# Scores and probability transposes of an attention kernel, from 64 x 64 and 128 x 128 array tiles to row tiles of 64 x 128

## The chip, the core and the metric

The kernel runs on one core of a Trainium2 chip. The metric is the device time of one execution in microseconds (us). The core has TensorE (PE; its weight loads are shown apart as PEld), VectorE (DVE), ScalarE (ACT), GpSimd (POOL) and the queue from which transfers are issued (SP). TensorE writes its results to PSUM, which has eight banks of 512 fp32 columns per partition; ACT and DVE copy them from there to SBUF.

## What is computed

```python
scores = (1.0 / np.sqrt(D)) * np.matmul(q, k.transpose(0, 1, 3, 2))   # B, H, S, D = 4, 8, 576, 64
bias = np.maximum((psi_rel / psi_i)[..., None] @ w1 + b1, 0.0) @ w2   # of the positions alone
scores = scores + bias.transpose(2, 0, 1)[None, :, :, :]
attn = np.exp(scores - np.max(scores, axis=-1, keepdims=True))
attn = attn / (np.sum(attn, axis=-1, keepdims=True) + 1e-09)
x = np.matmul(attn, v)                       # then (B * S, H * D) = (2304, 512)
h = x @ moe_w_in;  x = (h - np.tanh(h)) @ moe_w_out
h = x @ moe2_w_in; x = (s * np.maximum(h, 0.0) ** 2 + b) @ moe2_w_out
```

All of it is fp32.

## The kernel before

The program has three stages: the position bias (matmuls `b`, line 259), attention, and two feed-forward layers (matmuls `h`, line 312, and `a`, line 550). The change is in attention.

Attention works on 16 pairs (two heads of one batch). A pair `i` has five row blocks `t`: blocks 0 to 3 are 128 query rows of both heads, and block 4 is the last 64 rows of both heads, one head on partitions 0 to 63 and the other on 64 to 127. A loop over `n` runs 80 of these blocks (and three iterations more) as a pipeline that is written out by hand: iteration `n` emits the division of block `n - 2` by its sum (`emit_norm`, POOL, line 422, output `pn`), the scores of block `n` (`emit_score`, TensorE, line 383, output `s`), the exponentials of block `n - 1` (ACT, line 405), the bias and row minimum of block `n` (`emit_bias`, DVE, line 391), the reciprocal of block `n - 1` (DVE, line 413), the transposes of block `n - 3` (`emit_transpose`, TensorE, line 432, output `t`), their copies to `pt` (`emit_parts`, ACT and DVE, lines 444 to 451), some matmuls with the values (`emit_pv`, TensorE, line 462, output `o`), and at two of five iterations the copy of a finished `o` (DVE, line 469). Every engine runs its instructions in this order.

At 16 iterations a `weights_tick` is put at the end, which unpacks a piece of feed-forward weights: on DVE three instructions (lines 130, 139 and 142), on ACT two, on POOL one (line 87). They stand at these `n`:

```python
TK = [*range(15, 63, 4), 66, 70, 74, 78]
```

How the matmuls use the 128 x 128 array of TensorE:

- Scores of a head and row block: the contraction of 64 is split off as a row tile, the 576 keys are two halves of 288 that use the two row tiles (`c`), and the query rows go in two column tiles of 64. So four matmuls of 64 x 64 weights and 288 columns make a set that runs together. The trace shows two instructions for each fp32 matmul, so a head has two sets of four.
- Transposes: nine blocks of 128 x 128 of `pn`, which is the weight operand; the identity is the moving operand. Three blocks share a PSUM bank; there are three banks.
- Values: column tiles of 64, two heads side by side (128 x 64).

PSUM: two buffers of two banks for the scores, three banks for the transposes, one for `o`. A score tile can be written again when DVE has read it (line 391), a bank of the transposes when ACT or DVE has copied it.

Of the kernel before, what the change touches and what calls it, by code (L numbers as in the profile page):

```python
# [10 lines left out]
F32 = mybir.dt.float32  # L11
# [5 lines left out]
PSUM = bass.MemoryType.PSUM  # L17
DRAM = bass.MemoryType.DRAM

B, H, S, D = 4, 8, 576, 64  # L20
# [38 lines left out]
def tile_kernel(ctx, tc, qk, vd, wcat, wts, sb, ltab, psib, ipsi8, out):  # L59
    nc = tc.nc  # L60
# [13 lines left out]
    ident = const.tile([128, 128], F32, name="ident")  # L74
# [111 lines left out]
    with ExitStack() as c0:  # L186
# [40 lines left out]
        for n in range(NG + 2):  # L227
# [18 lines left out]
            if n < NG:  # L246
# [3 lines left out]
                f = 512 - y  # L250
# [85 lines left out]
    with ExitStack() as ca:  # L336
        sp = ca.enter_context(tc.tile_pool(name="sp", bufs=2, reuse_waits="tile"))
        pp = ca.enter_context(tc.tile_pool(name="pp", bufs=4, reuse_waits="tile"))
        np_ = ca.enter_context(tc.tile_pool(name="np_", bufs=3, reuse_waits="tile"))
        gp_ = ca.enter_context(tc.tile_pool(name="gp_", bufs=3))  # L340
        s_ctx = ExitStack()
        ps_s = s_ctx.enter_context(tc.tile_pool(name="ps_s", bufs=2, space=PSUM, side="right", reuse_waits="tile"))
        ps_t = ca.enter_context(tc.tile_pool(name="ps_t", bufs=3, space=PSUM, reuse_waits="tile"))
        ps_o = ca.enter_context(tc.tile_pool(name="ps_o", bufs=1, space=PSUM, reuse_waits="tile"))


# [3 lines left out]
        periods = [(i, t) for i in range(len(pairs)) for t in range(5)]  # L350
# [14 lines left out]
        s_t, raw_t, p_t, n_t, sums, tr_t, unit_t, o_t = {}, {}, {}, {}, {}, {}, {}, {}  # L365

        def heads_of(x):

            t = periods[x][1]
            return [(0, 8, 2)] if t == 4 else [(0, 2 * t, 0), (1, 2 * t + 1, 1)]  # L370

        def emit_score(x):
            i, t = periods[x]
            q, kk = qk_t[i]
            for j, _, e in heads_of(x):
                s = s_t[x, j] = ps_s.tile([128, 2, 512], F32, tag="s", name="s")
                for ee in ((e,) if e < 2 else (0, 1)):
                    o = s if e < 2 else s[ee * 64:ee * 64 + 64]
                    n = IT[t][1]
                    for c in range(2):  # L380
                        h = slice(c * 64, c * 64 + 64)
                        for r in range(0, n, 64):
                            nc.tensor.matmul(o[r:r + 64, c, 0:288], q[h, ee, t * 128 + r:t * 128 + r + 64], kk[h, ee],  # L383
                                             start=True, stop=True)

        def emit_bias(x):
            i, t = periods[x]
# [26 lines left out]

        def emit_norm(x):

            pn = n_t[x] = np_.tile([128, 9, 128], F32, tag="pn", name="pn").rearrange("p j n -> p (j n)")
            sm = sums.pop(x)
            for j, _, e in heads_of(x):
                p = p_t.pop((x, j))  # L420
                for a, b, c in ([(0, 512, 640), (512, 576, 576)] if j else [(0, 576, 0)]):
                    nc.gpsimd.tensor_scalar(out=pn[:, c:c + b - a], in0=p[:, a:b], scalar1=sm[:, j:j + 1],  # L422
                                            scalar2=0.0, op0=ALU.mult, op1=ALU.add)

        def emit_transpose(x):
            pn = n_t.pop(x)
            nb = 5 if periods[x][1] == 4 else 9
            for g in range(0, nb, 3):
                pm = tr_t[x, g] = ps_t.tile([128, 3, 128], F32, tag="t", name="t")
                for j in range(g, min(g + 3, nb)):  # L430
                    c = min(128, 128 * 4 + 64 - 128 * j) if nb == 5 else 128
                    nc.tensor.transpose(pm[0:c, j - g], pn[:, j * 128:j * 128 + c], ident)  # L432

        def emit_parts(x):

            i, t = periods[x]
            u = int(t > 1)
            if (i, u) not in unit_t:
                unit_t[i, u] = gp_.tile([128, 9, 320], F32, tag="pt", name="pt")
            pt = unit_t[i, u]  # L440
            if t < 4:
                c0 = t % 2 * 128
                for copy, g in ((nc.scalar.copy, 0), (nc.vector.tensor_copy, 3), (nc.scalar.copy, 6)):
                    copy(pt[:, g:g + 3, c0:c0 + 128], tr_t.pop((x, g)))  # L444
                return
            a, b = tr_t.pop((x, 0)), tr_t.pop((x, 3))
            for e, copy in ((0, nc.scalar.copy), (1, nc.vector.tensor_copy)):
                h = slice(e * 64, e * 64 + 64)
                copy(pt[:, 5 * e:5 * e + 3, 256:320], a[:, :, h])
                copy(pt[:, 5 * e + 3, 256:320], b[:, 0, h])  # L450
                copy(pt[h, 4, 256:320], b[0:64, 1, h])

        def emit_pv(i, u, j):

            r0, n = UNITS[u]
            v = v_t[i]
            if j == 0:
                o_t[i, u] = ps_o.tile([128, 512], F32, tag="o", name="o")[:, 0:n]
            o = o_t[i, u]
            for e in range(2):  # L460
                h = slice(e * 64, e * 64 + 64)
                nc.tensor.matmul(o[h], v[:, e, j], unit_t[i, u][:, 4 if j == 4 else 5 * e + j, 0:n], start=(j == 0), stop=(j == 4))  # L462

        def emit_out(i, u):
            hp, b = pairs[i]
            r0, n = UNITS[u]
            del unit_t[i, u]
            xo = sp.tile([128, 320], F32, tag="xo", name="xo", bufs=3)[:, 0:n]
            nc.vector.tensor_copy(xo, o_t.pop((i, u)))
            nc.sync.dma_start(out=x1_d[hp][:, b * S + r0:b * S + r0 + n], in_=xo)  # L470

# [10 lines left out]
        for n in range(NK + 6):  # L482
# [6 lines left out]
            if now(2):  # L489
                emit_norm(n - 2)  # L490
            if now(0):
                emit_score(n)
# [7 lines left out]
            if now(3):  # L500
                emit_transpose(n - 3)
                emit_parts(n - 3)
            for i, u, js in PV.pop(n, []):
                for j in js:
                    emit_pv(i, u, j)
                if js[-1] == 4:
                    emit_out(i, u)
# [13 lines left out]
    with ExitStack() as cb:  # L521
# [52 lines left out]
        for n in range(len(seq) + LAG):  # L574
# [15 lines left out]
            if n < len(seq):  # L590
                c, f = seq[n]
# [69 lines left out]
```

## Time and profile before

| what | us |
|---|---|
| median of 3 runs | 1104.89 (1104.89 to 1104.98) |
| span of the profiled execution, first to last instruction | 1102.9 |
| time around the span (median less span) | 2.0 |
| PE busy | 1091.7, 99% of the span |
| DVE busy | 635.9 (58%) |
| ACT busy | 484.4 (44%) |
| POOL busy | 319.9 (29%) |
| busy on scores (PE, line 383) | 89.9 |
| busy on transposes (PE, line 432) | 89.6 |
| busy on values (PE, line 462) | 95.0 |

The profiled execution is given by its span; its time from outside is not listed apart, and the median of the runs stands for it. Busy time of PE is the time in which some matmul is in flight, their ends included, so it says that TensorE had work, not that it was at its peak. The granted clock of TensorE was full (1.00, which is 2.4 GHz) in every window read here.

### The profile page before, as it was taken

The page shows a single profiled execution, that of the slowest core. Times are in us where ns is not written, and L with a number is a line of the kernel's source. Part 1 is how long each engine was busy: PE and PEld are TensorE (multiplying, and loading weights), DVE is VectorE, ACT ScalarE, POOL GpSimd, SP SyncE. Part 2 cuts the span into 40 slices and gives each one's busy share as a digit, 9 for nine tenths or more (in the row PEclk, how much of TensorE's full clock was granted, in tenths as well). Part 3 has the DMA queues.
Part 4 walks back from the last instruction along what each step waited for, and adds up shares of the span by engine and source line. Part 5 has one row for each costly group of instructions (what it writes and reads, how often), then busy time and mean ns, then how long its engine had stood idle before and what let it go on. Part 6 is the DMA issues. An engine that isn't in the chain of part 4 may idle for free.

```text
span 1102.9 us, 17963 instructions
## 1 busy us (share of the span) xinstructions
PE 1091.7 (99%) x6856; PEld 836.6 (76%) x6856; DVE 635.9 (58%) x1239; ACT 484.4 (44%) x1003; POOL 319.9 (29%) x438
## 2 busy tenths in 40 slices
PE   9999999999999999999999999999999999999998
PEld 6555555555578888889888888888888888888897
DVE  8866787787659942223322399998343343343343
ACT  8977777777735432222222255553222222222222
POOL 0155666676715530001200046435030020010000
PEclk9999999999999999999999999999999999999999
DMA  7957546253145010010100265600010020010010
GB/s 284 317 176 227 175 149 226 77 179 130 38 187 198 15 58 1 1 58 20 58 1 1 96 210 210 200 30 20 19 59 1 1 77 1 1 58 1 0 40 20
DMA packets 41335, 99.65 MB, mean 90 GB/s; under 512 B 5024, under 2 KB 11552, under 8 KB 41248
## 3 DMA queue, kind: packets, MB, share of 16 engines
q1 hardware_dynamic: 40960, 98.24, 26.2%
q8 instruction: 54, 0.88, 0.3%
q14 instruction: 33, 0.27, 0.1%
q10 hardware_dynamic: 288, 0.26, 0.1%
HBM read 73.41 MB, written 25.07 MB: 89 GB/s over the span
## 4 chain that ended last, share of the span: by engine, by line
PE 91%; DVE 2%; DMA 1%; issue 1%; ACT 0%; POOL 0%; SPq 0%; ACTq 0%; DVEq 0%
PE h L312 36%; PE a L550 36%; PE o L462 7%; PE t L432 6%; PE s L383 6%; DVE raw L391 1%; DMA qk<-in_qk 1%; DVE wx L142 0%; DVE wx L130 0%; ACT p L405 0%; DVE pt L444 0%; POOL pn L422 0%; DVE wsg L139 0%; SPq L111 0%; DVE mn L391 0%
## 5 line engine op out<-in xcount | busy, mean ns | idle before, releaser
L312 PE MATMUL h<-x,w 128*128 128x512 f32 (+1 forms) x1920 | 420.6, 368 | 0.0
L312 PEld LDWEIGHTS h<-x,w 128*128 128x128 f32 x1920 | 337.4, 188 | 62.4 <-issue 1.3
L550 PE MATMUL a<-ring,w 128*128 128x512 f32 (+1 forms) x960 | 210.1, 368 | 0.0
L550 PE MATMUL a<-w,ring 128*128 128x512 f32 x864 | 209.0, 389 | 0.0
L550 PEld LDWEIGHTS a<-ring,w 128*128 128x128 f32 x960 | 168.3, 189 | 29.9
L550 PEld LDWEIGHTS a<-w,ring 128*128 128x128 f32 x864 | 161.1, 188 | 32.7
L87 POOL TENSOR_TENSOR w<-wx,w 128x512 fp32r<-128x512 f32 x64 | 96.1, 1503 | 219.3 <-ACT w L122 212.4
L333 DVE TENSOR_TENSOR ring<-ring 128x512 fp32r<-128x512 f32 (+1 forms) x160 | 111.1, 695 | 78.8 <-ACT ring L332 78.8
L332 ACT CAST ring<-ring 128x512 fp32r<-128x512 f32 (+1 forms) x160 | 92.3, 577 | 137.9 <-DVE ring L327 98.7
L422 POOL TENSOR_SCALAR pn<-p,sm 128x576 f32<-128x576 f32 (+2 forms) x208 | 129.2, 638 | 43.7 <-DVE sm L413 31.7
L326 DVE TENSOR_TENSOR ring<-ring 128x512 f32<-128x512 f32 (+1 forms) x80 | 54.7, 684 | 147.7 <-ACT ring L325 147.6
L323 DVE TENSOR_TENSOR ring<-h,ring 128x512 f32<-128x512 f32 (+1 forms) x80 | 50.8, 634 | 140.2 <-ACT ring L322 140.1
L391 DVE CUSTOM_DVE_ANT_0 raw<-s,bias 128x576 f32<-128x576 f32 x144 | 103.7, 752 | 36.3 <-PE s L383 32.7
L84 POOL TENSOR_SCALAR x<-xr 128x512 fp32r<-128x512 f32 (+1 forms) x36 | 25.6, 711 | 330.5 <-DMA xr<-x_d 328.5
L322 ACT ACTIVATE ring<-h 128x512 f32<-128x512 f32 (+1 forms) x80 | 44.3, 554 | 164.7 <-PE h L312 164.7
L325 ACT ACTIVATE ring<-h 128x512 f32<-128x512 f32 (+1 forms) x80 | 44.4, 555 | 163.6 <-PE h L312 163.6
L405 ACT ACTIVATE p<-raw,mn 128x576 f32<-128x576 f32 x144 | 110.6, 770 | 6.1 <-DVE mn L391 5.7
L432 PEld LDWEIGHTS t<-ident,pn 128*128 128x128 f32 (+1 forms) x656 | 69.8, 140 | 36.0 <-issue 18.8
L462 PE MATMUL o<-pt,vv 128*64 128x256 f32 (+1 forms) x640 | 95.0, 418 | 0.0
L383 PE MATMUL s<-qk 64*64 64x288 f32 x1152 | 89.9, 418 | 4.6 <-DVE mn L391 4.1
L432 PE MATMUL t<-ident,pn 128*128 128x128 f32 (+1 forms) x656 | 89.6, 279 | 0.7 <-DVE pt L444 0.7
L444 ACT COPY pt<-t 128x384 f32<-128x384 f32 x128 | 60.3, 478 | 54.8 <-PE t L432 54.7
(48 smaller groups left out, 765.6 us busy)
## 6 DMA issues: line engine op xcount, KB each, us to landing
w<-in_wts SPq DMA_DIRECT2D x64, 512.0 KB, 4.7
qk<-in_qk SPq DMA_DIRECT2D x16, 864.0 KB, 5.9
bias_d<-m SPq DMA_DIRECT2D x36, 296.0 KB, 4.4
bias<-bias_d SPq DMA_DIRECT2D x32, 288.0 KB, 4.7
xr<-x_d SPq DMA_DIRECT2D x28, 256.0 KB, 3.0
vv<-in_vd SPq DMA_DIRECT2D x16, 320.0 KB, 3.7
x_d<-o SPq DMA_DIRECT2D x16, 256.0 KB, 2.1
out_x<-o SPq DMA_DIRECT2D x16, 256.0 KB, 2.1
```

The lines of the kernel that those rows point to most:

```text
L87: nc.gpsimd.tensor_tensor(out=lo, in0=raw, in1=hi.bitcast(F32), op=ALU.subtract)
L312: nc.tensor.matmul(h, a, x, start=(k == 0), stop=(k == 3 * KD - 1))
L332: nc.scalar.copy(gh, g)
L333: nc.vector.tensor_tensor(out=gl, in0=g, in1=gh.bitcast(F32), op=ALU.subtract)
L383: nc.tensor.matmul(o[r:r + 64, c, 0:288], q[h, ee, t * 128 + r:t * 128 + r + 64], kk[h, ee], start=True, stop=True)
L391: nc.vector.tensor_tensor_reduce(out=raw.rearrange("p (c j) -> p c j", c=2), in0=s_t.pop((x, j))[:, :, 0:288], in1=bias_t[pairs[i][0], k]. ...
L405: nc.scalar.activation(out=p, in_=raw, func=AF.Exp, scale=-1.0, bias=mn, accum_out=sm[:, j:j + 1])
L422: nc.gpsimd.tensor_scalar(out=pn[:, c:c + b - a], in0=p[:, a:b], scalar1=sm[:, j:j + 1], scalar2=0.0, op0=ALU.mult, op1=ALU.add)
L432: nc.tensor.transpose(pm[0:c, j - g], pn[:, j * 128:j * 128 + c], ident)
L444: copy(pt[:, g:g + 3, c0:c0 + 128], tr_t.pop((x, g)))
L462: nc.tensor.matmul(o[h], v[:, e, j], unit_t[i, u][:, 4 if j == 4 else 5 * e + j, 0:n], start=(j == 0), stop=(j == 4))
L550: nc.tensor.matmul(o, x, y, start=first and j == 0, stop=last and j == 2)
```

## The change

Three things change in attention.

- Scores of blocks 0 to 3: one matmul with 64 x 128 weights takes the place of two with 64 x 64, so a head has two sets of two matmuls. Block 4 keeps 64 x 64.
- Transposes: each block of `pn` is taken as two row tiles, rows 0 to 63 and rows 64 to 127. A transpose has 64 x 128 weights and 64 moving columns. The eight blocks of a row tile go to a bank of its own (`t0`, `t1`), and the two row tiles alternate. The ninth block (the last 64 keys of both heads) goes to a third bank `c`: the first row tile of two row blocks is transposed in the iteration of the second of them, the second row tile in the iteration after.
- Copies: ACT copies the whole bank of row tile 0 (512 columns), DVE that of row tile 1 (512 columns), ACT every second iteration 256 columns of `c`. Before it was 384 columns twice on ACT and once on DVE. POOL writes 64 columns more for block 4, `pn` has 5 buffers in place of 3, `xo` 2 in place of 3.

```diff
-        ps_t = ca.enter_context(tc.tile_pool(name="ps_t", bufs=3, space=PSUM, reuse_waits="tile"))
+        ps_t = ca.enter_context(tc.tile_pool(name="ps_t", bufs=1, space=PSUM, reuse_waits="tile"))
...
-                        for r in range(0, n, 64):
-                            nc.tensor.matmul(o[r:r + 64, c, 0:288], q[h, ee, t * 128 + r:t * 128 + r + 64], kk[h, ee],
-                                             start=True, stop=True)
+                        nc.tensor.matmul(o[0:n, c, 0:288], q[h, ee, t * 128:t * 128 + n], kk[h, ee], start=True, stop=True)
...
-                for a, b, c in ([(0, 512, 640), (512, 576, 576)] if j else [(0, 576, 0)]):
+                for a, b, c in ([(0, S, 0), (448, 512, S)], [(0, S, 0)], [(0, 512, 640), (512, S, S)])[(e + 1) % 3]:
...
+        ROWS = (slice(0, 64), slice(64, 128))
+        def turned(r, out_, in_):
+            nc.tensor.transpose(out_, in_, ident[ROWS[r], ROWS[r]])
+        def emit_tails(r, x):
+            if r == 0:
+                tr_t["c"] = ps_t.tile([128, 2, 2, 64], F32, tag="c", name="c")
+            for k in range(2):
+                turned(r, tr_t["c"][:, k, r], n_t[x + k][ROWS[r], 512:640])
         def emit_transpose(x):
-            for g in range(0, nb, 3):
-                pm = tr_t[x, g] = ps_t.tile([128, 3, 128], F32, tag="t", name="t")
-                for j in range(g, min(g + 3, nb)):
-                    c = min(128, 128 * 4 + 64 - 128 * j) if nb == 5 else 128
-                    nc.tensor.transpose(pm[0:c, j - g], pn[:, j * 128:j * 128 + c], ident)
+            if t in (1, 3):
+                emit_tails(0, x - 1)
+            ab = tr_t[x] = [ps_t.tile([128, 8, 64], F32, tag=f"t{r}", name=f"t{r}") for r in range(2)]
+            for j in range(8 if t < 4 else 5):
+                for r in range(2):
...
+                    turned(r, ab[r][:, j], pn[ROWS[r], c:c + 128])
+            if t in (2, 4):
+                emit_tails(1, x - 2)
...
-                for copy, g in ((nc.scalar.copy, 0), (nc.vector.tensor_copy, 3), (nc.scalar.copy, 6)):
-                    copy(pt[:, g:g + 3, c0:c0 + 128], tr_t.pop((x, g)))
+            for r, copy in ((0, nc.scalar.copy), (1, nc.vector.tensor_copy)):
+                if t < 4:
+                    copy(pt[:, 0:8, c0:c0 + 64], ab[r])
+                else:
+                    copy(pt[:, 4 * r:4 * r + 4, 256:320], ab[r][:, 0:4])
+                    copy(pt[ROWS[r], 8, 256:320], ab[r][ROWS[r], 4])
+            if t in (2, 4):
+                nc.scalar.copy(done[:, 8, 0:256], tr_t.pop("c").rearrange("p k r q -> p (k r q)"))
```

On TensorE this is one iteration before, with the transposes of a block of 128 rows and the scores of the next iteration behind them (an entry is a matmul of the program, the sizes are those of its output, and x is how many in a row).

```order
L383 MATMUL s<-qk 64x288 x8
L432 MATMUL t<-ident,pn 128x128 x9
L462 MATMUL o<-pt,vv 64x256 x4
L383 MATMUL s<-qk 64x288 x8
L432 MATMUL t<-ident,pn 128x128 x9
L462 MATMUL o<-pt,vv 64x256 x4
```

In the changed program the same place, from the last transposes of one iteration to the first of the next, reads as follows; `t_1108` and `t_1109` are the banks of row tile 0 and row tile 1 of one block, `t_1162` and `t_1163` those of the next.

```order
L426 MATMUL t_1108<-ident,pn 128x64
L426 MATMUL t_1109<-ident,pn 128x64
L426 MATMUL c<-ident,pn 128x64 x2
L481 MATMUL o<-pt,vv 64x256 x4
L382 MATMUL s<-qk 128x288 x4
L426 MATMUL c<-ident,pn 128x64 x2
L426 MATMUL t_1162<-ident,pn 128x64
L426 MATMUL t_1163<-ident,pn 128x64
```

The order of scores, transposes and values is as before; the scores are half as many, the transposes twice as many and alternate between two banks, and the `c` transposes come in twos on one row tile, behind the block in one iteration and ahead of it in the next.

On DVE an iteration before is the two bias instructions (`ISA raw,mn` and a read of the minimum), the reciprocal and one copy.

```order
L391 ISA raw,mn<-s,bias 128x576
L391 ISA mn 128x1
L391 ISA raw,mn<-s,bias 128x576
L391 ISA mn 128x1
L413 RECIPROCAL sm<-sm 128x2
L444 COPY pt<-t 128x3x128
```

After the change the same iteration on DVE has the larger copy, of the whole bank of row tile 1, at the same place behind the reciprocal.

```order
L389 ISA raw,mn<-s,bias 128x576
L389 ISA mn 128x1
L389 ISA raw,mn<-s,bias 128x576
L389 ISA mn 128x1
L411 RECIPROCAL sm<-sm 128x2
L464 COPY pt<-t_1421 128x8x64
```

Nothing moved on DVE but the size of the copy and the bank that it frees.

## Rows read from the trace of the kernel before

**Rows 1.** Windows: us; busy of PE, PEld, DVE, ACT, POOL; clock; DMA.

```profile
66.17:298.88 232.71, 229.24 (x2177) 128.08 (x2175) 176.93 (x497) 173.84 (x440) 154.39 (x278) 1.00 0.47 155
```

**Rows 2.** Timeline of PE, one pair: start us, duration us, what, count.

```profile
66.17 1.20 PE L383 MATMUL s<-qk 64*64 64x288 f32 x16
...
69.66 0.72 PE L383 MATMUL s<-qk 64*64 64x288 f32 x8
...
73.20 1.20 PE L383 MATMUL s<-qk 64*64 64x288 f32 x16
74.33 1.20 PE L432 MATMUL t<-ident,pn 128*128 128x128 f32 x9
75.47 1.08 PE L462 MATMUL o<-pt,vv 128*64 128x256 f32 x8
76.48 1.20 PE L383 MATMUL s<-qk 64*64 64x288 f32 x16
...
79.76 1.20 PE L383 MATMUL s<-qk 64*64 64x288 f32 x16
80.89 0.77 PE L432 MATMUL t<-ident,pn 128*128 128x128 f32 x5
81.58 0.65 PE L462 MATMUL o<-pt,vv 128*64 128x256 f32 x4
82.17 0.47 PE L383 MATMUL s<-qk 64*64 64x288 f32 x4
```

**Rows 3.** Tiles t, s, h: count, duration ns min/median/max, first and last start.

```profile
L432 PE MATMUL t<-ident,pn x583: 272/273/332, 67.3 to 297.5; 128*128 128x128 f32 x190, 128*64 128x128 f32 x5
...
L383 PE MATMUL s<-qk x1028: 402/403/453, 66.2 to 298.9; 64*64 64x288 f32 x172
...
L312 PE MATMUL h<-x,w x36: 387/390/499, 304.6 to 319.2; 128*128 128x512 f32 x36
```

**Rows 4.** Groups by form, weight loads: busy us, mean ns of one, idle.

```profile
L432 PEld LDWEIGHTS t<-ident,pn 128*128 128x128 f32 x640 | 68.5, 141 | 36.0 <-issue 18.8 <-POOL pn L422 10.1 <-POOL sm L409 3.9
...
L383 PEld LDWEIGHTS s<-qk 64*64 64x64 f32 x1152 | 35.4, 132 | 52.4 <-DVE mn L391 15.6 <-issue 12.4 <-DVE sm L413 6.3
...
L312 PEld LDWEIGHTS h<-x,w 128*128 128x128 f32 x24 | 4.3, 188 | 1.6 <-issue 0.8
...
L432 PEld LDWEIGHTS t<-ident,pn 128*64 128x64 f32 x16 | 1.8, 111 | 0.0
```

**Rows 5.** Timeline of PEld, the first loads of a score run.

```profile
256.90 0.15 PEld L383 LDWEIGHTS s<-qk 64*64 64x64 f32 x4 [0.38 <-issue]
```

**Rows 6.** Timeline of PE and PEld, transposes behind scores.

```profile
257.68 0.42 PE L383 MATMUL s<-qk 64*64 64x288 f32 x4
...
258.03 0.14 PEld L432 LDWEIGHTS t<-ident,pn 128*128 128x128 f32 x1 [0.44 <-issue]
```

**Rows 7.** Timeline of PE and PEld, transposes behind h.

```profile
307.22 0.39 PE L312 MATMUL h<-x,w 128*128 128x512 f32 x1
307.45 0.27 PE L432 MATMUL t<-ident,pn 128*128 128x128 f32 x1
...
307.22 0.14 PEld L432 LDWEIGHTS t<-ident,pn 128*128 128x128 f32 x1
```

**Rows 8.** Timeline of DVE around a tick, iterations 31 and 32.

```profile
144.11 0.54 DVE L444 COPY pt<-t 128x384 f32<-128x384 f32 x1
144.57 0.68 DVE L130 SCALAR_TENSOR_TENSOR wx<-wx,wsg 128x512 int32<-128x512 int32 x1
...
147.19 0.74 DVE L391 CUSTOM_DVE_ANT_0 raw<-s,bias 128x576 f32<-128x576 f32 x1
147.87 0.08 DVE L391 DVE_READ_ACCUMULATOR2_ANT mn<- 128x1 f32 x1
```

**Rows 9.** Timeline of PE, iteration 33; in brackets the idle time before.

```profile
148.00 1.40 PE L383 MATMUL s<-qk 64*64 64x288 f32 x16 [0.46 <-DVE mn L391]
```

**Rows 10.** Chain that ended last, 100 to 110 us, in order of time.

```profile
96.58 8.98 DMA qk<-in_qk
```

More of the change, by code (lines that the diff above doesn't have):

```diff
@@ L338, in tile_kernel @@
         pp = ca.enter_context(tc.tile_pool(name="pp", bufs=4, reuse_waits="tile"))
-        np_ = ca.enter_context(tc.tile_pool(name="np_", bufs=3, reuse_waits="tile"))
+        np_ = ca.enter_context(tc.tile_pool(name="np_", bufs=5, reuse_waits="tile"))
         gp_ = ca.enter_context(tc.tile_pool(name="gp_", bufs=3))
@@ L415, in emit_norm @@
         def emit_norm(x):
-            pn = n_t[x] = np_.tile([128, 9, 128], F32, tag="pn", name="pn").rearrange("p j n -> p (j n)")
+            pn = n_t[x] = np_.tile([128, 9 * 128], F32, tag="pn", name="pn")
             sm = sums.pop(x)
@@ L420, in emit_norm @@
                 p = p_t.pop((x, j))
-                for a, b, c in ([(0, 512, 640), (512, 576, 576)] if j else [(0, 576, 0)]):
+                for a, b, c in ([(0, S, 0), (448, 512, S)], [(0, S, 0)], [(0, 512, 640), (512, S, S)])[(e + 1) % 3]:
                     nc.gpsimd.tensor_scalar(out=pn[:, c:c + b - a], in0=p[:, a:b], scalar1=sm[:, j:j + 1],
                                             scalar2=0.0, op0=ALU.mult, op1=ALU.add)
-        def emit_transpose(x):
-            pn = n_t.pop(x)
-            nb = 5 if periods[x][1] == 4 else 9
-            for g in range(0, nb, 3):
-                pm = tr_t[x, g] = ps_t.tile([128, 3, 128], F32, tag="t", name="t")
-                for j in range(g, min(g + 3, nb)):
-                    c = min(128, 128 * 4 + 64 - 128 * j) if nb == 5 else 128
-                    nc.tensor.transpose(pm[0:c, j - g], pn[:, j * 128:j * 128 + c], ident)
+        ROWS = (slice(0, 64), slice(64, 128))
[6 more added lines that the diff above has]
+                turned(r, tr_t["c"][:, k, r], n_t[x + k][ROWS[r], 512:640])
+        def emit_transpose(x):
+            i, t = periods[x]
+            if t in (1, 3):
+                emit_tails(0, x - 1)
+            pn = n_t[x]
+            ab = tr_t[x] = [ps_t.tile([128, 8, 64], F32, tag=f"t{r}", name=f"t{r}") for r in range(2)]
+            for j in range(8 if t < 4 else 5):
+                for r in range(2):
+                    if t < 4:
+                        c = j * 128 + j // 4 * 128
+                    else:
+                        c = j * 128 if j < 4 else (512, 448)[r]
+                    turned(r, ab[r][:, j], pn[ROWS[r], c:c + 128])
+            if t in (2, 4):
+                emit_tails(1, x - 2)
+                del n_t[x - 2], n_t[x - 1]
+            if t == 4:
+                del n_t[x]
         def emit_parts(x):
@@ L440, in emit_parts @@
             pt = unit_t[i, u]
-            if t < 4:
-                c0 = t % 2 * 128
-                for copy, g in ((nc.scalar.copy, 0), (nc.vector.tensor_copy, 3), (nc.scalar.copy, 6)):
-                    copy(pt[:, g:g + 3, c0:c0 + 128], tr_t.pop((x, g)))
[L445 to L451, printed above, removed]
+            ab = tr_t.pop(x)
+            for r, copy in ((0, nc.scalar.copy), (1, nc.vector.tensor_copy)):
+                if t < 4:
+                    c0 = t % 2 * 128 + r * 64
+                    copy(pt[:, 0:8, c0:c0 + 64], ab[r])
+                else:
+                    copy(pt[:, 4 * r:4 * r + 4, 256:320], ab[r][:, 0:4])
+                    copy(pt[ROWS[r], 8, 256:320], ab[r][ROWS[r], 4])
+            if t in (2, 4):
+                done = unit_t[i, int(t == 4)]
+                nc.scalar.copy(done[:, 8, 0:256], tr_t.pop("c").rearrange("p k r q -> p (k r q)"))
         def emit_pv(i, u, j):
@@ L461, in emit_pv @@
                 h = slice(e * 64, e * 64 + 64)
-                nc.tensor.matmul(o[h], v[:, e, j], unit_t[i, u][:, 4 if j == 4 else 5 * e + j, 0:n], start=(j == 0), stop=(j == 4))
+                nc.tensor.matmul(o[h], v[:, e, j], unit_t[i, u][:, 8 if j == 4 else 4 * e + j, 0:n], start=(j == 0), stop=(j == 4))
         def emit_out(i, u):
@@ L467, in emit_out @@
             del unit_t[i, u]
-            xo = sp.tile([128, 320], F32, tag="xo", name="xo", bufs=3)[:, 0:n]
+            xo = sp.tile([128, 320], F32, tag="xo", name="xo", bufs=2)[:, 0:n]
             nc.vector.tensor_copy(xo, o_t.pop((i, u)))
```

## Prediction

> **What bounds the kernel now.** I read the busy times of the attention stage first: from 66.17 to 298.88 us PE is busy 229.24 of 232.71 us [rows 1]. So TensorE sets the time, and the other engines matter where it waits for them. The change touches attention alone; the feed-forward layers must take the time that they take now.
>
> Then I read one pair on PE, from 66.17 to 82.17 us, where nothing waits: 16.00 us [rows 2]. Its iterations take, from score start to score start, 3.28 (n mod 5 = 0: 73.20 to 76.48), 3.28 (1), 2.41 (2), 3.49 (3: 66.17 to 69.66) and 3.54 (4). Runs of different length give the steps within a run without their ends. Sixteen score instructions take 1.20 us and eight 0.72: a set of four is 0.24 us. Nine transposes take 1.20, five 0.77: 0.108 each. Eight value instructions take 1.08, four 0.65: 0.215 a set. An iteration of 3.28 us holds 4 x 0.24 + 9 x 0.108 + 4 x 0.215 = 2.79 us of this; the other 0.49 us lies between the runs, about 0.16 at each of three changes of tile shape.
>
> **Why a change of shape costs.** Behind scores, the first weight load of the transposes starts only at 258.03, 0.35 us after the last score set began at 257.68 [rows 6], though that set needs only 0.24. Behind `h`, which has the same 128 x 128 shape as the transposes, the load starts at 307.22 with the last `h` matmul, and the transpose at 307.45 [rows 7]; it loses nothing. So a run with the shape of the run before it starts without the 0.16.
>
> **The change, part by part.**
>
> *Shape.* Scores of blocks 0 to 3 and transposes get one shape. In the 77 iterations with both (n = 3 to 79) 16 have the scores of block 4, which stay 64 x 64. So 61 changes of shape go: 61 x 0.16 = -9.8 us. If transposing itself needs a switch, which no row separates, this is 0.
>
> *First load of the scores.* The first matmul of a run shows what of its weight load is not hidden, as its longest duration over the median: 0.050 us for scores with 64 columns (453 over 403), 0.109 for `h` with 128 (499 over 390), 0.059 for transposes with 128 (332 over 273) [rows 3]. A 64 x 128 score load is ordinary like that of `h`: +0.059 in 61 iterations, +3.6 us (0 if the load starts early). Later loads hide behind sets of 0.24. Half as many score matmuls gain nothing: sets are as long and as many, since the column tiles ran together.
>
> *Transposes.* The price is that of a slot, a pair of row tiles. The moving side is 64 columns, half of 128, so 0.054 of the 0.108. The load has 128 columns still. Loads of transposes are faster than others: 141 ns for 128 columns and 111 for 64 make 0.47 ns a column, whereas 188 for `h` and 132 for 64 columns of scores make 0.88 [rows 4]; 128 columns at 0.47 are 0.060 us, and the unhidden 0.059 says the same. Two loads on different row tiles overlap if they do as in the scores, where four loads (two row tiles by two column tiles) are in flight in 0.15 us [rows 5], hardly more than the 0.132 of one. So a slot is 0.060 us, bound by the load; ends are 0.054 and, with loads at the ordinary rate, 0.109. The two `c` transposes share a row tile and take a slot each. A pair has 8 + 10 + 10 + 10 + 7 = 45 slots: 2.70 us. Before it is 41 x 0.108 = 4.43. Gain 1.73 us, in 16 pairs -27.7.
>
> The section "LDWEIGHTS (loading the stationary operand)" of the page "TensorE: Matmul & The Clock Gate" of the Trainium skill speaks against this: a load takes its columns over 1.2 GHz, whatever its rows, which makes 107 ns here, an estimate from that page, and the sum of PE below about nothing. The rows on `h` agree with it, those on transposes do not.
>
> Sum on PE: -27.7 - 9.8 + 3.6 = -33.9 us, 2.13 a pair, which leaves 13.87. The iterations become 2.81 (0), 2.81 (1), 2.19 (2), 2.90 (3), 3.17 (4).
>
> *What is late next: DVE.* Each tick puts its instructions between the copy of an iteration and the bias of the next, 2.62 us (144.57 to 147.19) [rows 8]. Scores wait behind that for a PSUM buffer, and behind the scores everything on PE: at 148.00 TensorE had waited 0.46 us for the bias [rows 9], whose minimum was read at 147.87 [rows 8]. The stretch of [rows 1] holds 71 iterations, 14 pairs and one of 3.49 us more, which is 227.5 us without waits, so all waits today are 5.2 us. DVE is idle there for 55.8 us, 0.79 an iteration; shorter iterations take 0.43 of that and the larger copy 0.14, and each copying engine has one bank in place of three in turn. So the same tick is felt more. I worked one through by hand, that of iteration 31, counted from its score start. Bias starts at 0.83, each takes 0.68 (147.19 to 147.87), so both are done at 2.2; the reciprocal follows; the copy of 512 columns, for which I take 0.60 from 0.46 for 384 (144.11 to 144.57), ends at 2.87; the tick ends at 5.5. The first bias of iteration 32 ends at 6.2, and iteration 33's first score, due at 2.81 + 2.19 = 5.0, starts at 6.3: 1.3 us late. Its second score and its transposes, which wait for the second bias and for DVE's copy, add 0.3: 1.6 in all. The same by hand for the other places of a tick gives 2.4 at n mod 5 = 2 (2 ticks), 1.5 at 4 (4), 1.0 at 0 (3, without the first tick, which is only a part) and 0 at 3 (3); with three ticks at 1 that is 4.8 + 6.0 + 3.0 + 4.8 = 18.6 us, +13.4 to today's 5.2. Bounds: 4 (DVE's lateness partly absorbed) and 22 (ACT, which has two instructions in a tick, and POOL add their own).
>
> *Transfers.* The load of queries and keys for iteration 20 is issued at 96.58, at the end of iteration 16, and takes 8.98 us [rows 10]; the scores start when it lands. The stretch to there shrinks by up to 0.47 + 0.22 + 0.59 + 0.37 us, all of which turns into waiting: +1.5 us. Other such loads are issued into emptier queues; I count none. SP's order is as before.
>
> *At nothing:* ACT copies 640 columns an iteration in place of 768. POOL has 16 short instructions more; a `pn` is divided an iteration before it is transposed, and that iteration covers them; without it 16 x 0.3 us would show. Five `pn` buffers and two `xo` buffers are used at distances of five and two iterations.
>
> Net: -33.9 + 13.4 + 1.5 = -19.0. From the span of 1102.9 and 2.0 around it, 1104.9 as the median of the runs: **1085.9 us**.
>
> **Rivals.**
>
> 1. *Loads at the ordinary rate.* If a row-tile load takes 0.109 as for `h`, a slot is that: 45 x 0.109 = 4.91 us a pair, 0.48 more than today, +7.6 us. With -9.8 + 3.6 that is +1.4, and DVE stays covered: 1106, no change. This is the skill's rule above as a mechanism of this kernel. For it: `h` and scores; against it: both rows on transposes. 0.11.
> 2. *Row tiles do not overlap (other side).* Transposes might load one after the other: 82 loads. At 0.060 they take 4.92 us and the kernel 1106; at 0.109 they take 8.94, +72 us, and with -6.2 the time is 1171. PE alone is slower from a slot of about 0.107 us up. Against it the overlap in the scores [rows 5]; for it only that no run of before has row-tiled transposes. 0.07, of which 0.05 slower.
> 3. *Everything is given back.* If the single banks made PE wait for the copies in every iteration, by 0.2 us, 77 iterations cost 15 more: 1101. Against it: by the hand count the copy ends at 2.87 and the next transposes are due at 3.8. 0.06; a third of it ends slower or equal.
> 4. *Nothing is given back* by DVE: 1104.9 - 33.9 + 1.5 = 1072.5. Against it the wait in [rows 9], at longer iterations. 0.08.
>
> **Numbers.** The forecast has 0.68, with 1073 to 1098 as its own range (slot 0.054 to 0.068, give-back 4 to 22). The range of 8 in 10 reaches to rivals 4 and 1: 1069 to 1107. A difference under 0.2% (2.2 us) is about what a measurement of this kernel cannot tell from no change. Faster: 0.68 + 0.08 + 0.04 = 0.80; the same: 0.11 + 0.02 = 0.13; slower: 0.07.
>
> **What the changed profile would show.** Right: transposes start in pairs some 0.06 us apart, sixteen in about 0.7 us with their ends; their first load starts while the last score set runs; a pair without ticks takes about 13.9 us; PE's waits for the bias and for DVE's copies grow from a few us to over 10, after ticks. Wrong: slots of 0.11 (rival 1), of 0.12 or more (rival 2), waits for copies in iterations without a tick (rival 3), or a feed-forward stretch that got longer.

## The result, and the profile after

The changed kernel takes 1091.28 us (1090.64 to 1091.71, 4 runs) against 1104.89 for the kernel before: 13.6 us less, a ratio of 0.988 with a 95% interval of 0.986 to 0.989. The forecast was 1085.9, so the direction was right and the gain 5.4 us short.

The first thing to read is one pair in which nothing waits, on the timeline of PE in the changed kernel (start us, duration us, what, count).

```profile
66.03 1.24 PE L382 MATMUL s<-qk 64*128 64x288 f32 x8
67.10 0.66 PE L426 MATMUL t<-ident,pn 64*128 64x64 f32 x16
...
68.92 0.71 PE L382 MATMUL s<-qk 64*64 64x288 f32 x8
...
72.09 1.24 PE L382 MATMUL s<-qk 64*128 64x288 f32 x8
...
74.90 1.24 PE L382 MATMUL s<-qk 64*128 64x288 f32 x8
...
77.69 1.24 PE L382 MATMUL s<-qk 64*128 64x288 f32 x8
78.77 0.47 PE L426 MATMUL t<-ident,pn 64*128 64x64 f32 x10
...
79.88 0.51 PE L382 MATMUL s<-qk 64*128 64x288 f32 x2
```

From 66.03 to 79.88 the pair takes 13.85 us where it took 16.00 [rows 2]; the sum on PE said 13.87. Iterations take 2.89, 3.17, 2.81, 2.79 and 2.19. Sixteen transposes take 0.66 us and ten 0.47, so three pairs of row tiles take 0.19: 0.063 us a slot, where 0.060 was forecast.

The tiles' durations in the changed kernel (ns, min/median/max) give the loads.

```profile
L426 PEld LDWEIGHTS t<-ident,pn x1052: 134/138/226, 66.9 to 284.9; 64*128 64x128 f32 x176
...
L382 PEld LDWEIGHTS s<-qk x568: 129/186/187, 66.0 to 284.1; 64*128 64x128 f32 x152, 64*64 64x64 f32 x38
L382 PE MATMUL s<-qk x568: 402/403/507, 66.0 to 284.3; 64*128 64x288 f32 x152, 64*64 64x288 f32 x38
```

A load of 64 x 128 takes 138 ns for transposes and 186 for scores, as 128 x 128 loads took 141 (transposes) and 188 (`h`) [rows 4]. The first score matmul of a run shows 507 - 403 = 0.104 us of its load, where 0.109 was taken. And the shape: on the timeline of PEld and PE around 75.8 us, the first loads of the transposes stand in the middle of the last score set.

```profile
75.73 0.41 PE L382 MATMUL s<-qk 64*128 64x288 f32 x2
...
75.73 0.14 PEld L426 LDWEIGHTS c<-ident,pn 64*128 64x128 f32 x1
75.74 0.14 PEld L426 LDWEIGHTS t<-ident,pn 64*128 64x128 f32 x1
...
75.97 0.22 PE L426 MATMUL c<-ident,pn 64*128 64x64 f32 x1
```

The set starts at 75.73, the first loads of a `c` and of a `t` transpose start within 0.01 us of it and of each other, and the first transpose follows at 75.97, one set of 0.24 us later. Nothing is lost between the two runs, where before the load came only after the set [rows 6].

What was not as forecast is how much TensorE waits. These are the windows of the changed kernel over that pair and over the stretch from the scores of iteration 8 to those of iteration 79 (us, then busy us of PE, PEld, DVE, ACT, POOL, clock, DMA).

```profile
66.03:79.88 13.85, 13.85 (x164) 8.91 (x163) 10.54 (x32) 10.23 (x27) 8.83 (x19) 1.00 0.51 163
66.03:286.37 220.34, 204.94 (x2302) 127.55 (x2301) 185.35 (x485) 160.88 (x397) 160.63 (x290) 0.99 0.49 164
```

Fourteen pairs of 13.85 and one iteration of 2.89 are 196.8 us, so 23.5 of the 220.3 us are waits; before they were 5.2 of 232.7 [rows 1]. Waits are meant in this sense from here on: all time beyond that of iterations that nothing holds up. PE's row shows 15.4 us of the 23.5 as idle; the rest is runs of matmuls that are drawn out (the scores at 114.08 take 1.61 us and not 1.24), and about 1.4 us of it is a lower granted clock around iteration 49 (last section). DVE is busy 185.35 us where it was 176.93, mostly because its copies are larger (0.67 us for 512 columns, 0.54 for 384). Behind attention little changes: from the last scores to the end it is 802.9 us and was 804.0. Of the 13.6 us, 12.4 are in this stretch.

One place shows the mechanism, the tick at the end of iteration 27: DVE and then PE in the changed kernel.

```profile
124.01 1.49 DVE L130 SCALAR_TENSOR_TENSOR wx<-wx,wsg 128x512 int32<-128x512 int32 x1
125.42 0.41 DVE L139 TENSOR_SCALAR wsg<-w 128x512 int32<-128x512 int32 x1
125.76 1.15 DVE L142 SCALAR_TENSOR_TENSOR wx<-w,wx 128x512 int32<-128x512 int32 x1
126.83 0.74 DVE L389 CUSTOM_DVE_ANT_0 raw<-s,bias 128x576 f32<-128x576 f32 x1
127.50 0.08 DVE L389 DVE_READ_ACCUMULATOR2_ANT mn<- 128x1 f32 x1
...
128.26 0.67 DVE L464 COPY pt<-t 128x512 f32<-128x512 f32 x1
```

```profile
127.64 0.72 PE L382 MATMUL s<-qk 64*64 64x288 f32 x8 [1.73 <-DVE mn L389]
...
128.98 0.71 PE L426 MATMUL t<-ident,pn 64*128 64x64 f32 x15 [0.30 <-DVE pt L464]
```

The tick holds DVE from 124.01 to 126.83. The bias behind it ends at 127.50, and only then can the next scores be written: TensorE has stood for 1.73 us. The transposes behind stand again, until DVE has copied the bank of row tile 1.

### The profile page after: what moved, and what is told of

Its sections match the earlier page's. It is cut to its first block, busy times and chain, and to the rows that moved or that the text cites. A ratio compares the mean times of both kernels' runs of the same rounds, so it can differ in the third digit from the quotient of the medians.

```text
span 1089.3 us, 18185 instructions
## 1 busy us (share of the span) xinstructions
PE 1065.3 (98%) x7000; PEld 838.0 (77%) x7000; DVE 642.6 (59%) x1223; ACT 469.6 (43%) x955; POOL 327.5 (30%) x454
## 4 chain that ended last, share of the span: by engine, by line
PE 83%; POOL 4%; DVE 3%; DMA 2%; issue 2%; ACT 1%; ACTq 0%; SPq 0%; DVEq 0%; POOLq 0%
PE h L312 36%; PE a L569 36%; PE o L481 5%; PE s L382 4%; POOL pn L420 3%; PE t L426 2%; DMA qk<-in_qk 1%; DVE raw L389 1%; POOL w L87 1%; DVE pt L464 1%; DMA vv<-in_vd 1%; PE c L426 0%; POOL sm L407 0%; DVE wx L142 0%; DVE wx L130 0%
## 5 line engine op out<-in xcount | busy, mean ns | idle before, releaser
L420 POOL TENSOR_SCALAR pn<-p,sm 128x576 f32<-128x576 f32 (+2 forms) x224 | 136.8, 627 | 36.1 <-DVE sm L411 30.5
L382 PE MATMUL s<-qk 64*128 64x288 f32 (+1 forms) x640 | 93.8, 433 | 11.5 <-DVE mn L389 11.1
L382 PEld LDWEIGHTS s<-qk 64*128 64x128 f32 (+1 forms) x640 | 46.3, 175 | 55.7 <-DVE mn L389 24.4
L426 PEld LDWEIGHTS t<-ident,pn 64*128 64x128 f32 x1184 | 52.5, 140 | 16.8 <-DVE pt L464 6.0
L122 ACT CAST w<-wx 128x512 fp32r<-128x512 f32 x64 | 39.7, 621 | 58.8 <-DVE wx L142 57.7
```

The costliest lines, as they stand in the source:

```text
L382: nc.tensor.matmul(o[0:n, c, 0:288], q[h, ee, t * 128:t * 128 + n], kk[h, ee], start=True, stop=True)
L426: nc.tensor.transpose(out_, in_, ident[ROWS[r], ROWS[r]])
```

## The experiments

In the table a pair is the time of five iterations without waits, the stretch is that from iteration 8 to 79 in the profile of each kernel, and waits are the stretch less 14 pairs and one iteration of the kind n mod 5 = 3. The mean granted clock of the stretch is 0.99 in the changed kernel and with the copy ahead, 0.98 with the transposes alone and 1.00 in all others. The whole times are medians; the kernel before was 1104.8 to 1105.2 beside them.

| kernel | whole, us | ratio, 95% interval | pair | stretch | waits |
|---|---|---|---|---|---|
| before | 1104.89 | | 16.00 | 232.71 | 5.2 |
| changed | 1091.28 | 0.988 (0.986 to 0.989) | 13.85 | 220.34 | 23.5 |
| few ticks | 1096.2 (one run) | | 13.85 | 200.64 | 3.9 |
| transposes alone | 1095.44 | 0.991 (0.990 to 0.993) | 14.29 | 225.27 | 22.2 |
| scores alone | 1107.25 | 1.0017 (1.0008 to 1.0027) | 16.15 | 234.08 | 4.4 |
| changed, copy ahead | 1084.3 | 0.981 (0.979 to 0.982) | 13.85 | 216.33 | 19.6 |
| before, fewer value matmuls | 1082.79 (one run) | | 14.05 | 213.63 | 13.9 |
| changed, ticks at n mod 5 = 4 | 1080.73 | 0.978 (0.977 to 0.979) | 13.85 | 209.83 | 13.1 |
| before, ticks at n mod 5 = 4 | 1103.71 | 0.999 (0.998 to 1.000) | 16.00 | 230.85 | 3.4 |
| changed, copy ahead, half ticks | 1071.43 | 0.970 (0.968 to 0.971) | 13.85 | 201.63 | 4.9 |
| changed, half ticks | 1078.81 | 0.977 (0.975 to 0.978) | 13.85 | 207.26 | 10.5 |
| before, copy ahead, half ticks | 1099.32 | 0.995 (0.994 to 0.997) | 16.00 | 227.49 | 0.0 |

My theory is that the saving on TensorE is whole and that bursts of DVE's work, the ticks, give part of it back. The rivals are that the new copies and banks make TensorE wait whatever the ticks do, and that the amount of DVE's work counts and not where it stands.

**Few ticks.**

```diff
-TK = [*range(15, 63, 4), 66, 70, 74, 78]
+TK = [76, 77, 78, 79]
```

> The changed kernel with 4 of the 16 weight ticks in attention, all in its last four iterations; the rest of the unpacking falls into the feed-forward layers. If the ticks on DVE are what gave part of the gain back, every pair from the second to the fourteenth takes 13.84 us, as the second does in the changed kernel, and TensorE waits under 3 us in the 14 pairs in place of 23.7. If the single banks and the order of copies and reciprocals do it without ticks, at least 10 us of waits stay. The whole time is no test here: the unpacking that moves costs up to 22 us at the start of the feed-forward layers.

Every pair but three takes 13.85 us, to within 0.1 us, and 3.9 us of waits stay. PE's own waits in this stretch (us in total, times, longest):

```profile
PE s L382 <- DMA qk<-in_qk: 1.3, 1, 1.3
PE t L426 <- DVE pt L467: 0.9, 1, 0.9
PE s L382 <- DVE mn L389: 0.9, 1, 0.9
```

That is a little over the 3 us that the theory allowed, far under 10: without ticks the single banks make TensorE wait little. The first line is the transfer for iteration 20, for which 1.5 us had been forecast. The second is at iteration 63, where the reciprocal ahead of DVE's copy waits for POOL; the first tick of the end is the third. What moved into the feed-forward layers costs more there: from the last scores to the end it is 828.4 us. In the first 64 us of that PE has work for only 45 us, and the granted clock is 0.84:

```profile
265.98:330.00 64.02, 45.07 (x246) 32.05 (x247) 56.09 (x78) 30.56 (x58) 30.76 (x29) 0.84 0.42 164
```

**Transposes alone.**

```diff
-                        nc.tensor.matmul(o[0:n, c, 0:288], q[h, ee, t * 128:t * 128 + n], kk[h, ee], start=True, stop=True)
+                        for r in range(0, n, 64):
+                            nc.tensor.matmul(o[r:r + 64, c, 0:288], q[h, ee, t * 128 + r:t * 128 + r + 64], kk[h, ee],
+                                             start=True, stop=True)
```

> The row-tiled transposes with the scores of before (64 x 64). On TensorE the transposes give 27.7 us less, the change of shape stays, and the first score load stays hidden: a pair without waits takes 14.2 to 14.3 us. If DVE sets the time around ticks, less of what TensorE saves is given back than with the whole change, and the time is 1089 to 1093, near the whole change. If a wait of fixed size is added by the new copies whatever TensorE saves (18.5 us), it is 1096.

The pair is as expected, 14.29 us: -1.71 for the transposes, and the scores' new shape is worth 0.44 more. The time is not: 1095.4, near the 1096 of a fixed wait, and the waits are 22.2 us, hardly fewer than with the whole change. But part of that is the clock. The four runs lie between 1093.9 us at a mean granted clock of 0.998 and 1097.6 at 0.995, and the profiled one is the slowest. Its stretch and its iterations 29 and 49, and then iteration 29 of the changed kernel:

```profile
67.65:292.92 225.27, 211.57 (x2758) 114.13 (x2756) 184.97 (x483) 160.58 (x397) 160.16 (x291) 0.98 0.49 160
131.76:137.11 5.35, 5.05 (x39) 2.49 (x39) 2.71 (x8) 2.98 (x7) 4.11 (x10) 0.68 0.39 148
197.19:202.33 5.14, 4.83 (x39) 2.54 (x39) 2.72 (x8) 2.98 (x7) 4.05 (x10) 0.67 0.01 3
```

```profile
127.64:131.38 3.74, 3.44 (x38) 1.80 (x38) 2.71 (x8) 2.98 (x7) 2.74 (x7) 1.00 0.81 310
```

The same iteration takes 1.6 and 1.4 us more at the lower clock. Without that the waits are about 19.2 us here and 22.1 with the whole change, an estimate from these rows: 14.0 and 16.9 more than before, in the ratio 0.83. TensorE saves 1.71 us a pair here and 2.15 with the whole change, in the ratio 0.80. So this kernel does not speak for a wait of fixed size; what is given back can as well grow with what TensorE saves.

**Scores alone.** The kernel before with the new line of the scores.

> The scores of 64 x 128 with the transposes of before (128 x 128). The change of shape stays, and the first score load of an iteration is longer by 0.059 us: 61 times 0.059, +3.6 us, less what DVE's lateness hides of it: 1106 to 1109. If half as many score matmuls were worth something by themselves it would be under 1104.

1107.25, within the range. The pair is 0.15 us longer, 16 of which are 2.4 us, and the time is 2.2 us longer; the first load was priced at 0.24 a pair. Half as many score matmuls gain nothing; their shape pays only through the transposes behind them.

**Copy ahead of the reciprocal.** In the changed kernel:

```diff
-            if now(1):
-                emit_inverse(n - 1)
             if now(3):
                 emit_transpose(n - 3)
                 emit_parts(n - 3)
+            if now(1):
+                emit_inverse(n - 1)
```

> The changed kernel with the reciprocal of an iteration emitted behind the copies, so that DVE's copy no longer stands behind a reciprocal that waits for POOL's sum. If part of TensorE's waits for the copy come from that place in the order, they go (some 5 to 9 us with the loads' waits), and the time is 1082 to 1087. If only the amount of DVE's work counts, the time stays at 1090 to 1092.

1084.3, as expected for the first case: 7.0 us less than the changed kernel. What it removes is seen after the tick of iteration 23 in the changed kernel, where the hand count had no wait at all. POOL, DVE and PE there:

```profile
112.22 2.84 POOL L420 TENSOR_SCALAR pn<-p,sm 128x576 f32<-128x576 f32 x3
115.14 0.19 POOL L407 TENSOR_SCALAR sm<-sm 128x2 f32<-128x2 f32 x1
```

```profile
114.81 0.07 DVE L389 DVE_READ_ACCUMULATOR2_ANT mn<- 128x1 f32 x1
115.37 0.17 DVE L411 RECIPROCAL sm<-sm 128x2 f32<-128x2 f32 x1 [0.49 <-POOL sm L407]
115.45 0.67 DVE L464 COPY pt<-t 128x512 f32<-128x512 f32 x1
```

```profile
116.18 0.71 PE L426 MATMUL t<-ident,pn 64*128 64x64 f32 x15 [0.43 <-DVE pt L464]
```

POOL is late with its sum at 115.14, behind three divisions that take 2.84 us; the reciprocal holds DVE 0.49 us; the copy behind it frees the bank of row tile 1 late, and the transposes stand 0.43 us. With the copy ahead the waits behind this tick fall from 1.07 to 0.56 us. Waits in the stretch fall by 3.9 us, and the stretch begins at 65.04 instead of 66.03. The profiled execution, the slowest of the four at 1086.1 us, shows no more than that; the median is 1.8 us lower.

**Before, with fewer value matmuls.** It leaves out key blocks 1 and 2 in the product with the values, so the output lacks their part.

```diff
                 for j in js:
-                    emit_pv(i, u, j)
+                    if j not in (1, 2):
+                        emit_pv(i, u, j)
```

> The kernel before without the value matmuls of key blocks 1 and 2, which leaves out two fifths of the product with the values; three transpose banks, copies and scores as before. A pair without waits is 1.9 us shorter on TensorE, 14.1 us, close to the 13.85 of the changed kernel, and the shortening is spread over the same iterations. If shorter iterations are what makes the ticks on DVE felt, TensorE waits 17 to 24 us from the second to the last pair, and 1.0 us or so at iteration 25 and 45 as in the changed kernel. If the single bank for each copying engine and the larger copy do it, the waits stay at 5 to 9 us, with none at iterations 25 and 45.

This one came out between: 13.9 us of waits, with 0.5 us around iteration 25 and as much around 45. The kernel before has 5.2 and the changed one 23.5, so shorter iterations by themselves, with three banks and small copies, make 8.7 of the 18.3 us more. The other 9.6 belong to what else is new: one bank for each copying engine, 8.4 us more of DVE, and about 1.4 us of lower clock, which is full here. The division is rough: the iterations are not shortened alike (n mod 5 = 2 keeps its 2.41 us, and has 2.19 in the changed kernel), and 1.2 of the 13.9 us is the transfer for iteration 20. The copy's place behind the reciprocal is not new; that it costs more with one bank is argued, not shown.

**Ticks at another place**, in the changed kernel and in the one before.

```diff
-TK = [*range(15, 63, 4), 66, 70, 74, 78]
+TK = [*range(9, 80, 5)]
```

> The changed kernel with 15 weight ticks, one in each iteration with n mod 5 = 4 from 9 to 79, where a tick costs 0.9 us in the changed kernel in place of 1.1 to 2.4 elsewhere. If a tick costs what its place makes it cost, the waits are 15 x 0.9 plus 2 to 3 = 16 us in place of 23.7, and the time is 1082 to 1085. If the ticks cost the same wherever they stand, since DVE's work is what counts, it stays at 1090 to 1092.

> The kernel before with the same 15 ticks at n mod 5 = 4. There a tick costs 0.3 us at that place and 0.33 on the mean, so the time stays at 1104 to 1105.5. If the other places of the ticks gain by themselves, it is 1100 or less.

1080.7 in the changed kernel, 10.6 us less and a little better than expected, and 1103.7 in the one before, at the edge of no change. Waits fall to 13.1 us with the same unpacking in the stretch (13 of each of the three instructions on DVE), so the place counts and not the amount alone. In the changed kernel a tick costs most at the end of the iteration with five transposes and two value sets, the shortest (n mod 5 = 2, 2.4 us), and ahead of it (1, 2.3 us).

**Half ticks.** The ticks are cut in two, with the copy ahead of the reciprocal, then the cut alone, then both edits in the kernel before.

```diff
-TK = [*range(15, 63, 4), 66, 70, 74, 78]
+HEADS, TAILS = range(8, 80, 5), range(10, 82, 5)
...
-            for _ in range(TICKS.get(n, 0)):
-                weights_tick()
+            if n in HEADS:
+                tick_head()
+            if n in TAILS:
+                tick_tail()
```

`tick_head` is the cast, POOL's subtraction and the instruction of line 130; `tick_tail` the rest.

> The changed kernel with the reciprocal behind the copies and each tick cut in two: one DVE instruction with ACT's cast and POOL's subtraction at n mod 5 = 3, the two others with ACT's other one two iterations later. A half is some 1.2 us on DVE, against 0.36 us idle an iteration and 0.9 us by which DVE may be late. If bursts are the cause, waits fall to 4 to 9 us and the time to 1070 to 1077. If the amount of DVE's work is the cause, the waits stay near 19 and the time at 1083 to 1086.

> The changed kernel with the ticks cut in two, the reciprocal where it was, ahead of the copies. If the cut alone takes the bursts away, waits are under 8 us and the time is 1071 to 1075. If the place of the copy behind a reciprocal that waits for POOL costs by itself, as it seemed to by 7 us with whole ticks, the time is 1076 to 1080.

> The kernel before with the ticks cut in two and the reciprocal behind the copies. It has 5.3 us of waits to lose, so 1099 to 1102. If these two edits were worth more than that without the change, TensorE would not be what bounds it: under 1097.

With both edits the changed kernel takes 1071.4 us, 19.9 less than without them and 33.5 less than before. The stretch of this kernel:

```profile
64.69:266.32 201.63, 197.65 (x2302) 127.03 (x2300) 183.71 (x484) 161.16 (x397) 159.03 (x289) 1.00 0.54 179
```

DVE does as much as in the changed kernel, 183.7 against 185.4 us, in 201.6 us instead of 220.3, and PE waits 4.9. So the amount of DVE's work is not the cause; where and in what pieces it stands is. The cut alone gives 1078.8 with 10.5 us of waits: the place of the copy costs 7.4 us here too, and the expectation of under 8 us of waits for the cut alone fell. The halves also stand at other places than the whole ticks did, and whole ticks at n mod 5 = 4 had already given 1080.7: of the 12.5 us that the cut gives with the order kept, 1.9 are beyond that. Whole ticks at 4 with the copy ahead were not run, so how much is the cut and how much the place stays open. In the kernel before the two edits give 1099.3 and take all waits away. Under this order of DVE's work the change is worth 1099.32 - 1071.43 = 27.9 us, twice what it is worth as made.

## Why the prediction was right, and where not

- *Shape, -9.8 us.* Right. A pair with the new transposes and the old scores takes 14.29 us, with both 13.85; the 0.44 are about four changes of shape at 0.16 less four first loads at 0.05.
- *First load, +3.6.* Right in kind, 2.2 to 2.4 us by the kernel with the scores alone.
- *Transposes, -27.7.* Right: slot 0.063 us for 0.060, 16.00 - 14.29 = 1.71 us a pair for 1.73. Rivals 1 (0.109 a slot) and 2 (row tiles one after the other) are out by the same row. That the load bounds a slot, and not its 64 moving columns (0.054), no run separates. The Trainium skill's rule on loads (page "TensorE: Matmul & The Clock Gate", section "LDWEIGHTS (loading the stationary operand)"), columns over 1.2 GHz, makes 107 ns for 128 columns, an estimate; the scores' 0.104 us fits it, a slot of 0.063 us does not.
- *What is late next, +13.4.* The step that was mis-sized; the waits grew by 18.3 us. The hand count was 18.6 us of waits from ticks, and by place it was: 2.4 at n mod 5 = 2, measured 2.4 and, with the lower clock, 3.8; 1.6 at 1, measured 2.3; 1.5 at 4, measured 0.2, 0.9 and 0.9 (the fourth tick that was counted, at iteration 74, has no instruction on DVE in either trace); 1.0 at 0, measured 1.2 twice and 0.7; 0 at 3, measured 1.07. It let the reciprocal pass as soon as the bias was done. In the run it waits for POOL's sum, and DVE's copy behind it too; that is the wait after iteration 23, and at 62 and 63, where no tick stands, 2.0 us more (POOL is busy with the first feed-forward chunk). Putting the copy ahead gave 7.0 us back. From 18.6 to the 23.5 us measured it is +2.1 at 1, +1.3 at 2, +2.1 at 3, -4.1 at 4, and 3.4 where no tick had been counted. That the count came within 5 us is in part luck: what it had too much at 4 covers most of what it lacked elsewhere in the ticks. Of the 5.4 us by which the whole forecast was short, 3.1 are in the stretch and 2.3 outside of it, where 3.5 had been forecast and 1.2 came; that part was not followed.
- *Transfers, +1.5.* Wrong here, right in the mechanism: in the changed kernel iteration 20 waits 0.2 us, and the same load takes at most 7.6 us and not 8.98. Its length is not the whole reason: with few ticks it takes at most 7.4, and iteration 20 waits 1.3.
- Rival 3, waits for the copies in every iteration, is out by the kernel with few ticks. Rival 4, nothing given back, did not happen. That half ticks give 1071.4 where rival 4 said 1072.5 is chance: the same edits take the kernel before to 1099.3, and 27.9 of the 33.9 us arrive.

Open is how the 9.6 us that shorter iterations do not explain divide between the single bank and the larger copy. PSUM has no bank left for a second buffer, so that was not tried.

## What to carry to other kernels

When a bound engine gets faster by a seventh, as TensorE does here, read next what the other engines do in bursts: their mean load can stay under the bound while each burst is longer than the slack of one iteration. Before judging the change, move such work to where an iteration has slack, or cut it into pieces and spread them, and put the copy that frees a bank ahead of an instruction that waits for a third engine. Two runs of small matmuls are worth bringing to one array shape where the second can then load its weights under the first; the shape by itself earned nothing.

## What the runs showed of the hardware that was not expected

TensorE's granted clock fell after some waits and not after others. In the changed kernel it is 1.00 through the tick of iteration 47, in which PE stood 1.73 us, and lower right after it, while PE worked again; the windows:

```profile
187.20:190.84 3.64, 1.91 (x27) 1.01 (x23) 3.64 (x7) 2.16 (x6) 3.64 (x4) 1.00 0.39 126
190.84:193.20 2.36, 2.06 (x26) 1.39 (x26) 1.96 (x6) 1.63 (x4) 1.81 (x5) 0.72 0.00 0
193.20:196.00 2.80, 2.80 (x15) 1.16 (x14) 0.75 (x2) 1.35 (x3) 2.27 (x6) 0.63 0.00 0
196.00:199.00 3.00, 3.00 (x38) 2.16 (x38) 2.60 (x7) 1.25 (x3) 0.56 (x2) 1.00 0.42 105
```

A mean of 0.63 says that part of the stretch ran at the lower level, 1.2 GHz. This iteration, 49, takes 1.97 us more than without waits, where the same place after the like tick of iteration 27, at full clock, costs 0.57: 1.4 us for one fall. The wait alone does not decide it: PE stood 1.73 us after the tick of iteration 27 too, and the clock stayed at 1.00; with the transposes alone it fell after the like waits of both ticks. What decides stays open. In the kernel with half ticks the mean over the stretch is 1.00.

DVE's shift instruction of line 130 takes 0.68 us at 144.57 in the kernel before [rows 8], where POOL is idle until 145.23, and 1.49 us at 124.01 above, where POOL is at work throughout. POOL's being at work is not enough for it: line 142 takes 0.69 us at 139.14 in the changed kernel with POOL's division beside it. No experiment here separated this.
